# Twelve loads of v, each issued as two transfers: partitions 0 to 119 and partitions 120 to 127

## The chip, the cores and the metric

The kernel runs on one core of one Trainium2 chip. The metric is the device time of one execution in microseconds (us); lower is better. Beside the times there is one profiled execution, whose trace gives the start and length of every instruction, the issue and the completions of every DMA transfer, and what ended each wait.

## The reference, cut to what matters

Two stages follow each other. The first is a gated linear recurrence over 768 positions for each of 4 batches and 8 heads, with a state of 48 by 48. The second takes the result as 3072 tokens of width 384 through two matrix products with a gate g = h cos(h) between them.

```python
f = 1 / (1 + exp(-f_logit))
for t in range(S):                                    # S = 768, per batch and head
    state = f[t][:, None] * state + outer(k[t], v[t])
    y[t] = q[t] @ state
x = y.transpose(0, 2, 1, 3).reshape(3072, 384)
h = x @ w_in                                          # 384 -> 2048
out = (h * cos(h)) @ w_out                            # 2048 -> 384
```

q, k, v and f_logit are four f32 tensors of the same shape (4, 8, 768, 48). The output is 3072 by 384 in f32.

## The kernel before, in words

**Tiling.** The recurrence is cut into 12 pairs (the name n in the code): one pair is 256 positions of one batch, all 8 heads. Within a pair, position 2p + e of the 256 sits on partition p, e = 0 or 1. A load of one of the four inputs for a whole pair is therefore 128 partitions of 8 heads times 96 f32 numbers: on each partition eight runs of 384 bytes, 384 KB in all. For pairs 0 and 1 (HALVES) f, k and q come as two transfers of four heads each, 192 KB apiece; v always comes whole, since VHALVES is empty. The recurrence of a pair is turned into matrix products: running sums of the logarithms of f (step cum), decayed copies of q and k (qm, km), their transposes (qkt), scores (sc) with a mask (am), an inner part (y) and a part from the carried state (yi). After that, units m of 128 or 256 tokens go through the two products of the second stage (h, co, g, o, ot, out).

**What v feeds.** The load of v for pair n (step v*n*) has one reader, step vb*n* in line 400, which casts it to bf16 in the order that the products want. vb runs on ACT for pairs 0 to 2, on DVE for pairs 3 and 11 and on POOL for the others. Readers of vb are the four copies vt (line 404), which feed the inner part y (line 522), and the outer products ps (line 467), which feed the state (st, line 488, and sz, line 494).

**The order of the work.** Nothing is scheduled while the program is built. The string ORDER lists every step by name with its engine (T is PE, S is ACT, V is DVE, G is POOL, Y is SP) and the buffer that it takes; emit walks that list and calls each step. Each engine thus has its instructions in one fixed order and stops at the first whose semaphores are not there. SP only issues transfers: nearly all loads, all transposes of q and k by DMA (step tq, line 414, pairs 4 to 11) and nearly all stores, in one queue. A load whose buffer is still being read waits at the head of that queue with all later ones behind it. Each input has three buffers. Every transfer counts on one of eight completion semaphores, taken in turn over SP's and ACT's transfers, and a transfer waits at its issue for the one eight places before it; readers wait on the semaphore of the transfer that they read.

**Lines.** All loads of f, k, q and v are made by the helper load (lines 294 to 298), whose one DMA instruction stands under line 296. It calls G.step, which notes the name, the engines allowed, the function that issues the instruction and the tile it writes. The fetches of the weights stand in line 282 (step w) and their casts in line 196 (wc, by the helper copy), the first activation on f in line 329 (ex), the products with q and k in lines 337, 345 and 395, the gate of the second stage in line 552 and its products in lines 570 and 586, the stores in line 597.

Of the kernel before, what the change touches and what calls it, by code (L numbers as in the profile page):

```python
# [187 lines left out]
def describe(nc, cpool, ppool, q, k, v, f_logit, moe_w_in, moe_w_out, out):  # L188
    G = Graph()
    eng = lambda e: {"DVE": nc.vector, "POOL": nc.gpsimd, "ACT": nc.scalar, "SP": nc.sync}[e]  # L190
# [65 lines left out]
    p1, p2 = Banks("p1", tiles, 1), Banks("p2", tiles, 2)  # L256
# [36 lines left out]

    def load(name, val, src, b, c, h0, h1):
        tok = src[b, h0:h1, 2 * C * c:2 * C * c + 2 * C, :] if nc is not None else None
        G.step(name, ("SP", "ACT"), lambda e: eng(e).dma_start(  # L296
            out=val.ap.rearrange("p h e d -> p h (e d)"),
            in_=tok.rearrange("h (p e) d -> p h (e d)", e=2)), writes=[val])

    def fetch(kind, pool, src, n, b, c, cut):  # L300

        whole = Val(pool)
        hs = [whole.part(lambda a, u=u: a[:, 4 * u:4 * u + 4]) for u in range(2)]
        if cut:
            for u in range(2):
                load(f"{kind}{n}.{u}", hs[u], src, b, c, 4 * u, 4 * u + 4)
        else:
            load(f"{kind}{n}", whole, src, b, c, 0, H)
        return whole, hs
# [390 lines left out]
```

## Time and profile before

| What | Value |
|---|---|
| Median of 3 runs | 194.66 us |
| The three runs | 196.32, 194.66, 190.06 us |
| The profiled execution | 190.06 us |
| Its span in the trace | 188.3 us |
| Granted TensorE clock, mean | 0.994 |
| Transfers issued | 98 by SP, 6 by ACT |
| Bytes moved by DMA | 34.47 MB in 74395 packets, 67456 of them under 512 B |
| Loads of v | 12 of 384 KB, all by SP, from 2.3 us to 127.8 us |
| Issue of a load of v, min / median / max | 0.379 / 0.943 / 3.577 us |
| Issue to landing of a load of v, min / median / max | 5.3 / 6.5 / 8.1 us |

The profiled execution is the fastest of the three runs. Its span is 1.8 us shorter than its time: what lies around the first and the last instruction. The three runs are 3.3% apart.

How to read what follows: PE is the matrix engine, DVE, ACT and POOL are the three engines for element-wise work, SP the one that issues transfers. SPq is SP's queue: the length of an issue in the trace includes the wait of that instruction for room or for a semaphore, so that an issue of 3.5 us need not be 3.5 us of work. "Landing" is the sixteenth of a transfer's completions: in the trace before, each transfer reports sixteen, at times of their own. An idle time "<- X" was ended by X.

### The profile page before, as it was taken

How to read it: one execution, taken by the hardware profiler on the slowest of the kernel's cores; microseconds unless marked ns; L12 is line 12 of the kernel's file. 1: busy time of each engine (PE TensorE's matmuls, PEld its weight loads, DVE VectorE, ACT ScalarE, POOL GpSimd, SP SyncE). 2: the span in 40 equal slices, each digit the busy share in tenths (PEclk: the TensorE clock that was granted, in tenths of full speed). 3: DMA queues.
4: the chain of work that ended last, by engine and by line, in shares of the span. 5: the costliest groups of instructions: out<-in, count | busy, mean ns of one | idle time of the engine just before them, and what ended most of it. 6: DMA issues, size and time to landing. Idle time of an engine off the chain costs nothing.

```text
span 188.3 us, 5965 instructions
## 1 busy us (share of the span) xinstructions
PE 172.6 (92%) x2523; PEld 123.4 (66%) x2527; DVE 150.0 (80%) x208; ACT 130.7 (69%) x183; POOL 100.6 (53%) x129
## 2 busy tenths in 40 slices
PE   7898658999997999999998999989998999999990
PEld 2464447976666875678566886657667888666660
DVE  4289997998969999898989999989996978633101
ACT  2988775799778899988966989766656774603030
POOL 4538699764498986986457990877833000000000
PEclk9999999999999999999999999999999999999997
DMA  6999999978999599999899899939652000020144
GB/s 146 261 261 270 354 342 309 289 207 244 263 247 253 141 221 255 194 219 209 157 279 282 222 248 201 250 84 166 93 139 87 3 0 0 3 84 0 42 150 146
DMA packets 74395, 34.47 MB, mean 183 GB/s; under 512 B 67456, under 2 KB 72832, under 8 KB 74368
## 3 DMA queue, kind: packets, MB, share of 16 engines
q1 hardware_dynamic: 70944, 32.71, 74.9%
q10 hardware_dynamic: 3424, 1.38, 3.0%
q8 instruction: 20, 0.33, 0.8%
q14 instruction: 7, 0.06, 0.1%
HBM read 25.17 MB, written 4.72 MB: 159 GB/s over the span
## 4 chain that ended last, share of the span: by engine, by line
DVE 40%; PE 36%; DMA 8%; issue 6%; ACT 4%; SPq 3%; POOL 2%; DVEq 0%; ACTq 0%; POOLq 0%
PE ps L570 18%; PE ps L586 14%; DVE am L449 10%; DVE g L552 10%; DVE vt L196 5%; DVE sz L494 4%; DVE st L488 4%; DMA f<-in_f_logit_dram 3%; DMA qkt<-qk 3%; DMA out_dram<-ot 2%; SPq L296 2%; PE ps L522 2%; DVE q L337 2%; DVE qkt L196 1%; DVE x L196 1%
## 5 line engine op out<-in xcount | busy, mean ns | idle before, releaser
L586 PE MATMUL ps<-w_out_bf,g 128*128 128x384 bf16 x384 | 67.9, 327 | 0.4 <-DVE g L552 0.4
L570 PE MATMUL ps<-x,w_in_bf 128*128 128x256 bf16 (+1 forms) x624 | 66.8, 265 | 1.0 <-DVE x L196 0.5
L575 ACT ACTIVATE co<-ps,halfpi 128x1024 bf16<-128x1024 f32 x48 | 52.6, 1113 | 21.7 <-PE ps L570 19.7
L552 DVE TENSOR_TENSOR g<-ps,co 128x1024 bf16<-128x1024 f32 x48 | 60.2, 1303 | 7.9 <-ACT co L575 7.8
L570 PEld LDWEIGHTS <-w_in_bf 128*128 128x128 bf16 x624 | 56.4, 98 | 9.1 <-issue 1.5
L586 PEld LDWEIGHTS <-g 128*128 128x128 bf16 x384 | 36.0, 98 | 23.0 <-DVE g L552 1.2
L449 DVE TENSOR_TENSOR am<-ps,pmask 128x1024 bf16<-128x1024 f32 x24 | 28.6, 1216 | 1.7 <-PE ps L445 0.9
L395 POOL TENSOR_TENSOR qk<-q,b 128x384 bf16<-128x384 f32 x19 | 19.0, 1005 | 8.5 <-DVE q L337 8.3
L395 POOL TENSOR_TENSOR qk<-k,bi 128x384 bf16<-128x384 f32 x21 | 21.7, 1044 | 2.8 <-ACT b L382 1.0
L196 ACT COPY ot<-ps 128x384 f32<-128x384 f32 (+1 forms) x17 | 7.7, 459 | 18.8 <-PE ps L586 9.8
L494 POOL TENSOR_TENSOR sz<-st,b 64x192 bf16<-64x192 f32 x21 | 12.9, 613 | 9.7 <-DVE st L488 8.0
L264 PE MATMUL ps<-zero 128*128 128x512 bf16 x49 | 14.3, 425 | 1.6 <-DVE zero L202 1.2
L196 DVE COPY ot<-ps 128x384 f32<-128x384 f32 (+1 forms) x9 | 4.5, 505 | 12.7 <-PE ps L586 12.3
L345 POOL TENSOR_TENSOR k<-k,f 128x384 f32<-128x384 f32 (+1 forms) x12 | 11.3, 940 | 6.3 <-ACT f L341 4.0
L354 POOL TENSOR_TENSOR sp<-ls 128x384 bf16<-128x384 f32 x8 | 8.0, 1010 | 9.9 <-ACT ls L333 5.0
L488 DVE TENSOR_TENSOR st<-ps,sz 64x192 f32<-64x192 f32 x32 | 11.3, 354 | 1.3 <-issue 0.4
L329 ACT ACTIVATE f<-f 128x768 f32<-128x768 f32 (+1 forms) x14 | 10.4, 748 | 2.2 <-DMA f<-in_f_logit_dram 2.0
L196 DVE COPY vt<-vb 64x384 bf16<-64x384 bf16 x18 | 11.3, 633 | 0.3
L522 PE MATMUL ps<-am,vt 128*32 128x128 bf16 x384 | 7.9, 220 | 3.1 <-DVE am L449 1.6
L445 PE MATMUL ps<-qkt 48*64 48x128 bf16 x384 | 9.2, 220 | 1.6 <-DVE st L488 1.1
L196 POOL COPY vt<-vb 64x384 bf16<-64x384 bf16 x17 | 9.2, 540 | 1.7 <-POOL qk L395 0.9
L445 PEld LDWEIGHTS <-qkt 48*64 48x64 bf16 x384 | 6.2, 106 | 5.2 <-DVE st L488 1.6
(65 smaller groups left out, 178.6 us busy)
## 6 DMA issues: line engine op xcount, KB each, us to landing
v<-in_v_dram SPq DMA_DIRECT2D x12, 384.0 KB, 6.5
out_dram<-ot SPq DMA_DIRECT2D x22, 192.0 KB, 3.3
q<-in_q_dram SPq DMA_DIRECT2D x10, 384.0 KB, 5.8
f<-in_f_logit_dram SPq DMA_DIRECT2D x9, 384.0 KB, 5.7
k<-in_k_dram SPq DMA_DIRECT2D x9, 384.0 KB, 6.1
g<-in_moe_w_in_dram SPq DMA_DIRECT2D x4, 768.0 KB, 7.7
g<-in_moe_w_out_dram SPq DMA_DIRECT2D x4, 768.0 KB, 7.3
k<-in_k_dram SPq DMA_DIRECT2D x4, 192.0 KB, 4.9
```

The lines of the kernel that those rows point to most:

```text
L196: (nc.scalar.copy if e == "ACT" else eng(e).tensor_copy)(out=o, in_=i)
L264: G.step(f"zf{i}", ("PE",), lambda e, dump=dump: nc.tensor.matmul(dump.ap, lhsT=zero[:, 0:128], rhs=zero, start=True, stop=True), writes=[ ...
L395: G.step(f"{nm}{n}.{u}", ("POOL", "DVE"), lambda e, u=u, j=j, src=src, dec=dec: eng(e).tensor_mul(out=qkp[u][j].ap[:, :, :, 0:D], in0=swap ...
L445: nc.tensor.matmul(o[t, r, 2 * a + g, :].rearrange("p (e n) -> p e n", e=2), lhsT=qkv(u)[s, 1, a, g, x, :], rhs=qkv(u)[s, 0, a, g, :, :], ...
L449: G.step(f"am{n}.{u}", ("DVE",), lambda e, u=u, sc=sc: nc.vector.tensor_mul(out=am[u].ap.rearrange("p r b n -> p (r b) n"), in0=sc.ap.rear ...
L488: nc.vector.tensor_add(out=st.ap[s], in0=view()[s], in1=S0.ap[s, :, r, :])
L494: eng(e).tensor_mul(out=new.ap[s, :, r, :].rearrange("p (u a) n -> p u a n", u=2), in0=ap()[s].rearrange("p (u a) n -> p u a n", u=2), in1 ...
L522: nc.tensor.matmul(py[g].ap[32 * c:32 * c + 32, C * m:C * m + C], start=(py[g].first and (g, c) not in begun), stop=(py[g].final and left[ ...
L552: nc.vector.tensor_mul(out=o.rearrange("p b (n e) -> p b e n", e=2), in0=ph.ap.rearrange("p (b e n) -> p b e n", e=2, n=64), in1=co.ap.rea ...
L570: nc.tensor.matmul(ph.ap[:, i * T:(i + 1) * T].rearrange("p (g t) -> p g t", t=C), lhsT=w_in_bf[:, kk, f0:f0 + 128], rhs=xa[:, :, kk, :], ...
L575: G.step(f"co{m}.{j}", ("ACT",), lambda e, ph=ph, co=co: nc.scalar.activation(out=co.ap, in_=ph.ap, func=AF.Sin, bias=halfpi), reads=[ph], ...
L586: nc.tensor.matmul(po.ap[:, 0:DM], lhsT=gT.ap[:, j, i * C:(i + 1) * C], rhs=w_out_bf[:, j, :], start=(po.first and j == 4 * s), stop=(po.f ...
```

## The change

Each load whose step's name begins with v is issued as two DMA instructions one after the other, the first for partitions 0 to 119 and the second for partitions 120 to 127. Both run on the engine that the step has in ORDER, which is SP for all twelve. All other loads stay one instruction over 128 partitions. The tile, its buffers, the bytes and the order of the steps stay as they were; SP's queue has 12 more transfers. Each reader of v now has two completions to wait for instead of one, and the turn of the eight semaphores moves on by two places for a load of v.

```diff
     def load(name, val, src, b, c, h0, h1):
         tok = src[b, h0:h1, 2 * C * c:2 * C * c + 2 * C, :] if nc is not None else None
-        G.step(name, ("SP", "ACT"), lambda e: eng(e).dma_start(
-            out=val.ap.rearrange("p h e d -> p h (e d)"),
-            in_=tok.rearrange("h (p e) d -> p h (e d)", e=2)), writes=[val])
+        parts = ((0, 120), (120, 128)) if name[0] == "v" else ((0, 128),)
+
+        def fill(e):
+            for p0, p1 in parts:
+                eng(e).dma_start(out=val.ap.rearrange("p h e d -> p h (e d)")[p0:p1],
+                                 in_=tok.rearrange("h (p e) d -> p h (e d)", e=2)[p0:p1])
+        G.step(name, ("SP", "ACT"), fill, writes=[val])
```

## The prediction

> **What bounds the kernel now.** I read the page's busy times and chain first, then the stretches, because a share over the span mixes stages; then SP's queue and the tile v, which the change touches. Busy times, DMA busy by slice, DMA queues, the chain by engine, and the issues of v:
>
> ```profile
> PE 172.6 (92%) x2523; PEld 123.4 (66%) x2527; DVE 150.0 (80%) x208; ACT 130.7 (69%) x183; POOL 100.6 (53%) x129
> ...
> DMA  6999999978999599999899899939652000020144
> ...
> q1 hardware_dynamic: 70944, 32.71, 74.9%
> ...
> q8 instruction: 20, 0.33, 0.8%
> ...
> DVE 40%; PE 36%; DMA 8%; issue 6%; ACT 4%; SPq 3%; POOL 2%; DVEq 0%; ACTq 0%; POOLq 0%
> ...
> v<-in_v_dram SPq DMA_DIRECT2D x12, 384.0 KB, 6.5
> ```
>
> The chain runs over DVE and PE; DMA has 8% of it. Yet the transfer engines are at nine tenths for two thirds of the span. The same by stretches (span, then busy time of PE, PEld, DVE, ACT, POOL, the clock, the DMA share and GB/s):
>
> ```profile
> 0.00:62.00 62.00, 53.59 (x871) 36.73 (x876) 51.33 (x89) 48.19 (x76) 42.09 (x57) 1.00 1.06 266
> 62.00:95.00 33.00, 32.42 (x476) 23.96 (x475) 31.66 (x38) 30.29 (x39) 24.98 (x32) 1.00 1.03 196
> 95.00:125.00 30.00, 28.59 (x455) 20.80 (x453) 28.79 (x41) 23.22 (x33) 21.61 (x25) 1.00 1.03 240
> 125.00:145.00 20.00, 19.02 (x444) 14.15 (x441) 17.53 (x23) 13.66 (x20) 11.96 (x16) 1.00 0.58 114
> ```
>
> To 62 us transfers are the scarcest thing beside DVE; from 62 to 125 us DVE and PE are at 95% and more; after 145 us PE is the busy one (38.98 of 43.3 us by the last row, not shown), and no load is left. All loads of v fall before 128 us. The tile v (issues, then who waited for its landing, then issue to landing):
>
> ```profile
> L296 SPq DMA_DIRECT2D v<-in_v_dram x12: 379/943/3577, 2.3 to 127.8; - x12
> ...
>   DMA v<-in_v_dram: 0.2, 1
> ...
>   POOL vb L196: 0.2, 1
> ...
> DMA to landing us min/median/max: 5.3/6.5/8.1
> ```
>
> Only 0.2 us of idle time in the whole span was ended by v itself. And the longest waits of SP's queue to 62 us (total, times, longest):
>
> ```profile
> SPq L282 <- ACT w_out_bf L196: 5.1, 1, 5.1
> SPq L296 <- POOL sp L354: 4.6, 1, 4.6
> SPq L296 <- ACT co L575: 3.0, 1, 3.0
> ```
>
> SP waits for buffers to come free, not for time to issue.
>
> **The issues added.** Twelve transfers on SP. An issue with nothing in its way costs 0.38 us (the shortest of v) to 0.51 us (v0, at 2.33 us); at 0.45 us that is 5.4 us of SP's time. What hides it, load by load from SP's timeline: v0, v1, v3, v4 and v6 are issued while the transfers are the limit: 384 KB land every 1.45 us (48.08, 49.59, 51.09 us), and 5.3 to 8.1 us from issue to landing means three to five transfers queued ahead. After v2 SP waits from 36.8 to 41.9 us for the weights' buffer; after v5 from 59.9 us to 64.4 us for the first transpose; after v7 a store waits for its output until 78.4 us, and the transpose behind it for POOL until 82.9 us. After v8 to v10 the transpose tq8.0 waits for POOL until 110.75 us, and stores ahead of it for DVE until 108.8 us. After v11 tq10.0 waits for POOL until 130.63 us, 1.2 us after its issue. Cost taken: nothing; without that cover 0.45 us each, 5.4 us in all.
>
> The added wait is that of a transfer for the one eight places before it. With v counted twice, eight places hold fewer bytes. I counted places in SP's order against the landings: the tightest are the second part of v9 (waits for k9, landed 98.13 us, due about 98.9 us) and q4 (for v3, 49.59 us, due 50.8 us). Nothing stops; if one did, all of SP's queue behind it would. The second semaphore at vb is a wait of 17 to 30 ns as the trace's other ones are: nothing.
>
> **The transfers themselves.** The bytes and runs of 384 bytes are the same. Does a split cost? The halves of f, k and q (192 KB) land 0.73 to 0.77 us apart (9.14, 9.90, 10.65, 11.42 us), whole loads 1.45 to 1.5 us: time goes with bytes, and two halves cost no more than one whole. So the lower bound by rows is nothing. The upper bound is that the smaller transfer is dealt as badly as can be, and the larger one too, so that some engine carries twice its share: 1.45 us a load. Between them I take one row more on the fullest engine: 128 rows over 16 engines are 8 rows in 1.45 us, a ninth row is 0.18 us. It is near the row of the halves, yet not nothing: a half has 128 rows of four heads and spreads as evenly as a whole, which 120 and 8 rows need not do. A gain is possible only if an engine that is late gets less; that is a rival below.
>
> *By the Trainium skill, page "DMA: Bandwidth & Descriptors", section "Why a DMA increments its semaphore by 16 and not by 1", a transfer runs on the largest number of engines up to 16 that divides its slowest dimension, the lowest-numbered ones: 15 for 120 rows and 8 for 8. Engines 0 to 7 would then carry nine rows, 8 to 14 eight, and the last none, which gives the same 0.18 us; no transfer of before has a count other than 128, so no run here shows it. The same page's "Rules for kernel authors" speaks against the change: disjoint partition ranges share the same engines, and one transfer of 128 partitions is advised; by it the sum is not below nothing.*
>
> **Who feels 0.18 us.** I set each landing of v beside the start of its vb. Seven loads have slack: v2 3.91, v3 1.26, v4 2.16, v6 4.44, v7 2.59, v9 4.35, v10 0.68 us. Four do not: v1 0.20, v5 0.07, v8 0.05, v11 0.09 us; v0 has 0.30 us, but f1.0 two transfers behind it is the chain itself (landing 9.90 us, activation 9.92 us). What queues behind these vb: on ACT the exponentials and tables of the next pair, on POOL qm and km, on DVE (v11) a stretch without idle time to 141 us. Counting all five in full: 5 x 0.18 = 0.9 us. That is generous for v5 and v8, since POOL has 2% of the chain.
>
> Sum, against the profiled execution: 190.06 + 0.9 = 191.0 us. That execution is the fastest of three; set on their median, 194.66 + 0.9 = **195.6 us**, 0.5% slower. I predict on the median. The three runs lie 3.3% apart, so 2% either way is about what can be told from no change.
>
> **Rivals.**
> *The late engine is spared (faster).* After an instruction fetch (q8, 16 KB packets, 1.16 us in the mean) one engine lags: fifteen completions of k1.1 are in by 15.84 us, the last at 17.25 us; for v5 64.10 and 65.23 us; for v8 103.20 and 104.34 us. If the engine that v leaves free is that one, it catches up 1.45 us a load, and the transfers behind land with the rest. For: the fetches take 20 x 1.16 = 23 us of it, v 12 x 1.45 = 17 us, near balance. Against: which engine lags is not in the trace, and the readers concerned sit on POOL. Worth at most the lags where a reader stood ready, 1.41 (k1.1) + 0.96 (w0.3) + 0.84 (k3) + 1.13 + 1.14 = 5.5 us; I take a third, 1.8 us: 192.9 us, down to 189.2. By the skill's rule above it is the sixteenth engine that v leaves free. Chance 0.20, half of it beyond 2%.
> *Fewer engines than I think (slower).* If 120 rows are not dealt out in eights but over 8 engines, those carry 15 or 16 rows, and a load of v takes 2.9 us. It decides from the second load on, where transfers are the limit: the five loads without slack at 1.45 us give 7.3 us, 202.0 us; half of it, where POOL absorbs, 198.3. For: the dealing is unseen. Against: the even landing of all 128-row transfers, which gives no sign of a costly dealing. Chance 0.18.
> *SP becomes the limit (slower).* Half of the 5.4 us of issues reach the path, at the transposes that share the queue: the chain waits for one in full (133.03 us, 4.87 us, qkt). 195.6 + 2.7 = 198.3 us. Against: the waits listed above. Chance 0.15, two thirds of it beyond 2%.
> *The change does nothing* (each vb waits for something else): 194.7 us; it is in my forecast.
>
> **How the numbers follow.** Forecast 0.47, of which 0.34 within 2%, 0.06 faster and 0.07 slower by the scatter of the runs. Faster 0.06 + 0.10 = 0.16; slower 0.07 + 0.18 + 0.10 = 0.35; within 2% the rest, 0.49. The forecast's own range is 190.06 + 0.9 to 196.32 + 0.9: 191.0 to 197.2 us. The range goes down to 190.5 us (most of the spared engine) and up to 200.5 us (SP, and the cheaper half of fewer engines), leaving out about 2 in 10.
>
> **What would show it.** SP's view of the load line: 24 issues of v, unblocked ones at 0.4 to 0.5 us; if some stay over 1 us at the second part, room in the queue is what is short. Transfers of v landing 0.2 us later against their neighbours confirm the ninth row, 1.4 us the fewer engines; a last completion no longer late by a microsecond behind a fetch, the spared engine. The idle time ended by v should stay under 1 us. I am wrong if waits "SPq <- DMA" appear, if ACT or DVE waits for v by microseconds, or if the transposes land later than 5 us.

## The result and the profile after

| | Before, measured beside it | After |
|---|---|---|
| Median | 190.15 us (19 executions) | 194.99 us (19 executions) |
| Lowest to highest | 189.18 to 196.32 us | 191.00 to 198.56 us |
| Ratio after / before | | 1.0113, 95% interval 1.0068 to 1.0157 |
| Profiled execution, its span | 190.06 us, 188.3 us | 197.03 us, 195.3 us |
| Granted TensorE clock, mean | 0.994 | 0.982 |

The ratio leaves out executions far above the quickest of their own kernel, of which after has many more than before. By the ratio the change costs 1.1%, some 2.1 us; by the medians 4.8 us. The profile after lies in the upper part of its times, so I read it for what can go wrong, and a second profile of the same kernel (192.57 us) beside it. The changed file is four lines longer: L296 is now L300, and L467, L494, L552 and L570 are L471, L498, L556 and L574.

The page of the changed kernel: busy times, the granted clock and the DMA share in 40 slices, the transfer queue (packets, MB, share of 16 engines), the chain by engine, and the issues of v (count, KB, us to landing).

```profile
PE 177.1 (91%) x2527; PEld 126.3 (65%) x2527; DVE 153.6 (79%) x208; ACT 131.2 (67%) x183; POOL 100.1 (51%) x129
...
PEclk9999988999998899999999999999999999999999
DMA  6999999976999999996389999995956000020152
...
q1 hardware_dynamic: 71028, 32.71, 75.7%
...
PE 37%; DVE 28%; DMA 21%; POOL 4%; ACT 3%; issue 3%; SPq 1%; DVEq 0%; ACTq 0%; POOLq 0%
...
v<-in_v_dram SPq DMA_DIRECT2D x12, 360.0 KB, 7.6
```

The same bytes move, but DMA's share of the chain has gone from 8% to 21%, and the larger part of v lands 7.6 us after its issue (the median) where whole loads took 6.5. The clock row has two dips, at slices 6 and 7 and at 13 and 14. The same by stretches (columns as in the prediction: span, busy times, clock, DMA share, GB/s):

```profile
0.00:62.00 62.00, 53.52 (x848) 35.95 (x849) 49.69 (x83) 47.15 (x74) 39.29 (x53) 0.97 1.07 248
62.00:95.00 33.00, 29.94 (x426) 22.68 (x427) 30.78 (x38) 24.82 (x33) 23.62 (x30) 0.95 0.91 196
95.00:125.00 30.00, 28.75 (x436) 21.18 (x437) 27.78 (x36) 25.72 (x33) 19.35 (x24) 1.00 1.06 206
```

To 62 us the transfer engines are as busy as before (1.07 against 1.06) and move 248 GB/s in place of 266. PE lost 2.5 us of work between 62 and 95 us (29.94 against 32.42 us busy). The tile v (issues, then what ended the idle time before its readers, who waited for it, and issue to landing):

```profile
L300 SPq DMA_DIRECT2D v<-in_v_dram x24: 295/882/3814, 2.3 to 136.2; - x24
...
  DMA v<-in_v_dram: 4.2, 5
...
  PE ps L471: 2.5, 2
  ACT vb L196: 2.4, 2
  POOL vb L196: 1.9, 3
...
DMA to landing us min/median/max: 5.9/7.6/9.9
```

The last line holds only the parts whose completions the view can count off; read from all completions, the twelve 120-row parts take 5.0 to 9.9 us, with the same median of 7.6. Before, 0.2 us of idle time in one place was ended by v; now 4.2 us in five. SP's own waits to 62 us, by contrast, have hardly moved (total, times, longest), and no wait of SP's for a transfer is among the longest:

```profile
SPq L282 <- ACT w_out_bf L196: 6.1, 1, 6.1
SPq L300 <- POOL sp L358: 4.1, 1, 4.1
SPq L300 <- ACT f L333: 2.5, 2, 1.4
SPq L300 <- ACT co L579: 1.8, 1, 1.8
```

**Landings**, read from the completions in the two traces, in us; both parts must have landed:

| Transfer | v0 | q0.0 | f1.0 | v1 | k1.1 | v2 | v3 | v4 | v6 | v5 | v8 |
|---|---|---|---|---|---|---|---|---|---|---|---|
| Before | 8.41 | 9.14 | 9.90 | 15.14 | 17.25 | 39.71 | 49.59 | 55.42 | 56.72 | 65.23 | 104.34 |
| After | 9.28 | 9.84 | 10.60 | 17.75 | 18.20 | 42.40 | 53.14 | 59.89 | 62.19 | 69.85 | 112.79 |

q0.0 and f1.0, the whole transfers behind the first split one, are each 0.70 us late. That is four times the 0.18 us of the prediction, by the first load alone.

**Where the time came in.** The end of the first, 10th, 16th, 25th and 46th of the 48 gates on DVE (g, L556), in us, in the traces of these kernels (the last two are experiments below):

| Profile | 1st | 10th | 16th | 25th | 46th | Time |
|---|---|---|---|---|---|---|
| Before | 33.1 | 64.6 | 83.0 | 110.0 | 163.6 | 190.06 |
| After | 35.2 | 68.8 | 90.2 | 117.2 | 171.0 | 197.03 |
| The changed kernel again | 31.8 | 67.0 | 86.2 | 113.2 | 166.8 | 192.57 |
| After, one multiply moved | 33.6 | 66.1 | 84.8 | 111.8 | 165.9 | 192.48 |
| The same, TensorE's gaps filled | 32.7 | 65.5 | 84.1 | 111.1 | 165.4 | 191.16 |

The whole loss of after is there by the 16th gate: 2.1 us by 33 us, 2.1 more by 69 us, 3.0 more by 90 us. Behind that the two kernels run in step.

### The profile page after: what moved, and what is told of

Its sections match the earlier page's. It is cut to its first block, busy times and chain, and to the rows that moved or that the text cites. A ratio compares the mean times of both kernels' runs of the same rounds, so it can differ in the third digit from the quotient of the medians.

```text
span 195.3 us, 5981 instructions
## 1 busy us (share of the span) xinstructions
PE 177.1 (91%) x2527; PEld 126.3 (65%) x2527; DVE 153.6 (79%) x208; ACT 131.2 (67%) x183; POOL 100.1 (51%) x129
## 4 chain that ended last, share of the span: by engine, by line
PE 37%; DVE 28%; DMA 21%; POOL 4%; ACT 3%; issue 3%; SPq 1%; DVEq 0%; ACTq 0%; POOLq 0%
PE ps L574 18%; PE ps L590 12%; DMA v<-in_v_dram 8%; DVE g L556 8%; DVE am L453 6%; DMA qkt<-qk 6%; DMA f<-in_f_logit_dram 5%; DVE sz L498 4%; DVE vt L196 4%; DMA out_dram<-ot 3%; POOL qk L399 2%; PE ps L264 2%; DVE st L492 2%; ACT co L579 2%; PE ps L449 1%
## 5 line engine op out<-in xcount | busy, mean ns | idle before, releaser
L574 PE MATMUL ps<-x,w_in_bf 128*128 128x256 bf16 (+1 forms) x624 | 69.9, 272 | 1.0 <-DVE x L196 0.6
L556 DVE TENSOR_TENSOR g<-ps,co 128x1024 bf16<-128x1024 f32 x48 | 60.2, 1303 | 9.4 <-ACT co L579 9.3
L574 PEld LDWEIGHTS <-w_in_bf 128*128 128x128 bf16 x624 | 58.7, 101 | 10.1 <-issue 1.8
L498 POOL TENSOR_TENSOR sz<-st,b 64x192 bf16<-64x192 f32 x21 | 12.1, 575 | 12.6 <-DVE st L492 8.5
L264 PE MATMUL ps<-zero 128*128 128x512 bf16 x53 | 16.1, 439 | 1.2 <-DVE zero L202 1.2
L196 DVE COPY vt<-vb 64x384 bf16<-64x384 bf16 x18 | 11.8, 662 | 0.3
L498 DVE TENSOR_TENSOR sz<-st,b 64x192 bf16<-64x192 f32 x11 | 11.9, 1082 | 0.2
```

What stands on the lines that cost most here:

```text
L196: (nc.scalar.copy if e == "ACT" else eng(e).tensor_copy)(out=o, in_=i)
L264: G.step(f"zf{i}", ("PE",), lambda e, dump=dump: nc.tensor.matmul(dump.ap, lhsT=zero[:, 0:128], rhs=zero, start=True, stop=True), writes=[ ...
L498: eng(e).tensor_mul(out=new.ap[s, :, r, :].rearrange("p (u a) n -> p u a n", u=2), in0=ap()[s].rearrange("p (u a) n -> p u a n", u=2), in1 ...
L556: nc.vector.tensor_mul(out=o.rearrange("p b (n e) -> p b e n", e=2), in0=ph.ap.rearrange("p (b e n) -> p b e n", e=2, n=64), in1=co.ap.rea ...
L574: nc.tensor.matmul(ph.ap[:, i * T:(i + 1) * T].rearrange("p (g t) -> p g t", t=C), lhsT=w_in_bf[:, kk, f0:f0 + 128], rhs=xa[:, :, kk, :], ...
```

## Experiments: is it the second transfer, or leaving out partitions?

My theory at this point: a transfer that leaves partitions out takes longer than its bytes. The rivals: SP's extra issue and the second semaphore cost the time, or one engine carries a ninth row.

**The changed kernel again**, for a profile at another granted clock.

> The changed kernel once more, beside the two other splits below on the same chip. Measured so far: 1.0113 of the kernel before (0.7% to 1.6% slower), where 1.005 was forecast. Three theories. Engine count: the 120-row transfer, on 15 engines, moves its rows more slowly than a 128-row transfer on 16 does (in the trace of the changed kernel q0.0 and f1.0, behind v0, land 0.70 us later than before, not 0.18). Second issue: it is the second transfer as such, its issue of 0.4 us in SP's queue and its place among the eight semaphores. Ninth row: a load costs 0.18 us as forecast, and the rest is scatter. All three expect 1.007 to 1.016 here, that is 191.5 to 193.5 us beside 190.2 us; the profile should show q0.0 landing about 9.8 us again, against 9.14 us before.

Measured: median 193.44 us (10 executions, 188.88 to 197.81) against 189.74 us of before; ratio 0.9999 (0.9945 to 1.0053). Its profile took 192.57 us at clock 1.00, q0.0 landing at 9.87 us. So the late landing repeats, but the ratio does not, and its interval does not overlap that of the result: it differs from call to call by as much as the 1.1% that it showed. The medians lie above before in both calls, by 4.8 and 3.7 us.

**Split at 64, and at 112.**

```diff
-        parts = ((0, 120), (120, 128)) if name[0] == "v" else ((0, 128),)
+        parts = ((0, 64), (64, 128)) if name[0] == "v" else ((0, 128),)
```

> Each load of v as partitions 0 to 63 and 64 to 127: the second issue and the semaphore places stay, but both parts can use 16 engines with four rows each. Engine count and ninth row expect the time of before, 0.998 to 1.003, and q0.0 landing at 9.1 to 9.3 us. Second issue expects what the changed kernel has, 1.007 to 1.016.

> Each load of v as partitions 0 to 111 and 112 to 127: one large and one small part as in the change, but seven rows and one row on each of 16 engines. Engine count expects 0.998 to 1.003, if it is the 15 engines that cost; if any transfer that isn't a power of two of rows is slow, the 112 rows take longer than 1.3 us and the ratio lies at 1.005 to 1.016. Second issue expects 1.007 to 1.016. Ninth row expects 0.998 to 1.003.

Measured: 194.16 us (188.30 to 199.19, 10 executions) and 195.44 us (190.78 to 198.13, four executions) against 189.74 us. q0.0 lands at 9.64 and 9.45 us, 0.50 and 0.31 us behind before. Both are as slow as the split at 120. Every part of these two reports sixteen completions, and 112 rows are seven for each of 16 engines, 64 are four; so the loss needs neither a ninth row nor an engine left out.

**The same bytes in two transfers of all 128 partitions**, heads 0 to 3 and heads 4 to 7.

```diff
-        parts = ((0, 120), (120, 128)) if name[0] == "v" else ((0, 128),)
+        parts = ((0, 4), (4, 8)) if name[0] == "v" else ((0, h1 - h0),)
...
-            for p0, p1 in parts:
-                eng(e).dma_start(out=val.ap.rearrange("p h e d -> p h (e d)")[p0:p1],
-                                 in_=tok.rearrange("h (p e) d -> p h (e d)", e=2)[p0:p1])
+            for a0, a1 in parts:
+                eng(e).dma_start(out=val.ap.rearrange("p h e d -> p h (e d)")[:, a0:a1],
+                                 in_=tok.rearrange("h (p e) d -> p h (e d)", e=2)[:, a0:a1])
```

> Each load of v as two transfers of all 128 partitions, heads 0 to 3 and heads 4 to 7 (192 KB each): the second issue and the turn of the semaphores are those of the change, but no transfer leaves out partitions. So far: the change, 64 and 64 rows, and 112 and 16 rows all have a median of 193 to 195 us beside 189.7 us, so that the number of engines alone isn't it. Theory partial rows: a transfer of fewer than 128 partitions takes more than its share of the queue (alone: 1.21 us for 128 rows, 1.62 us for 120, 1.85 us for 120 and 8, 1.67 us for 64 and 64); it expects the time of before here, median 189 to 191 us, and q0.0 landing at 9.1 to 9.3 us. Theory second issue: SP's queue and the semaphores; it expects 193 to 196 us.

Measured: 190.37 us (189.28 to 191.85, 12 executions) against 190.57 us, ratio 1.0002 (0.9962 to 1.0042). The tile v and the clock of this run:

```profile
L300 SPq DMA_DIRECT2D v<-in_v_dram x24: 375/653/3210, 2.3 to 128.3; - x24
...
  DMA v<-in_v_dram: 1.3, 2
...
DMA to landing us min/median/max: 3.2/5.2/6.9
```

As many issues, as many semaphores and turns as in the changed kernel, and no loss. v0 lands at 8.17 and q0.0 at 8.92 us, 0.2 us ahead of before. SP's issues are cleared; the cost lies in leaving partitions out.

**Transfers alone.** Loads of the same sources and shapes in groups of six, with nothing else running but a copy per tile that keeps the groups apart.

> The transfers by themselves, with no compute but a copy that frees each buffer: groups of six loads of 128 rows, 120 rows (0 to 119), 112 rows, 8 rows, 120 and 8 rows, 64 and 64 rows, 120 rows (8 to 127) and 64 rows. None of the reference's computation is done. It gives the time from one landing to the next in a full queue. Engine count expects 1.45 us for 128 rows, 2.0 to 2.3 us for 120 rows, 1.3 us for 112 rows, 2.1 to 2.4 us for 120 and 8, 1.45 us for 64 and 64. Ninth row expects 1.45 us for 120 rows, 1.6 us for 120 and 8. If 120 rows from partition 8 on are as slow as from 0, it is the number of engines, and not which partitions they hold.

> Transfers alone again, none of the computation is done: groups of six loads of 128 rows, two transfers of four heads each, 112 and 16 rows, 120 and 8, 120, 104, 88, 96 and 32 rows. 104 and 88 rows fill 13 and 11 engines with eight rows each, as 120 rows fill 15. If each engine is slow by itself (eight rows that aren't spread as in a 128-row transfer), 120, 104 and 88 rows all take 1.6 us; if the engines hinder each other, fewer rows take less: 104 rows 1.4 us, 88 rows 1.2 us. Two transfers of four heads take 1.2 to 1.25 us a load; 112 and 16 rows 1.5 to 1.7 us, as 64 and 64 did.

Measured, from landing to landing within a group, where the steps are steady (the first and last of some groups are longer):

| Rows in one load | First run | Second run |
|---|---|---|
| 128 | 1.21 us | 1.21 us |
| 128, two transfers of four heads | | 0.60 us each, 1.21 us |
| 120 + 8 | 1.82 to 1.99 us | 1.86 us |
| 112 + 16 | | 1.55 us |
| 64 + 64 | 0.83 us each, 1.67 us | |
| 120 | 1.62 us | 1.49 to 1.63 us, median 1.58 |
| 120, rows 8 to 127 | 1.54 to 1.76 us | |
| 112 | 1.25 us | |
| 104 | | about 1.4 us |
| 96 | | 1.40 us |
| 88 | | 1.2 to 1.5 us |
| 64 | 1.04 us | |
| 32 | | 0.2 to 0.5 us |
| 8 | 0.2 to 0.6 us | |

In the second run's page the rate in 40 slices of 2.33 us shows the step: whole loads and loads by heads first, then 112 + 16, and from the 13th slice on 120 + 8 and the other partial ones. The 365 GB/s near the end are stores.

```profile
DMA  1999999999999999999999986789999941999994
GB/s 18 294 325 321 323 324 324 308 261 251 254 219 222 220 229 219 219 231 227 223 211 220 228 191 186 218 195 211 219 210 197 120 88 59 365 368 368 365 366 166
```

The engines report themselves as busy until the loads of 88 rows, at 325 GB/s with whole loads and at some 220 with 120 rows. So a split load costs 1.86 - 1.21 = 0.65 us, of which some 0.3 us is the smaller transfer itself (1.86 - 1.58). What inside the transfer engines makes 120 or 96 rows slower than 128 stays open: 104 and 88 rows go to fewer engines (thirteen and eleven completions) and take less time than 120, so it is not the number of engines alone, and no run here shows which partitions each engine is given.

**Only the first three, and only the last nine.**

```diff
-        parts = ((0, 120), (120, 128)) if name[0] == "v" else ((0, 128),)
+        parts = ((0, 120), (120, 128)) if name in ("v0", "v1", "v2") else ((0, 128),)
```

> Only v0, v1 and v2 are split at 120, the other nine are whole. In the change everything is 0.7 us late from 10 us on and 2.2 us late at 42 us. If the early loads are what counts, since transfers are the limit there, about half to two thirds of the loss is here: median 191.5 to 194 us, and vb1 again 2 us later than before (15.34 us). If the loss comes from the loads after 42 us, 189.5 to 190.5 us.

> Only v3 to v11 are split at 120, the first three are whole. If the early loads are what counts: median 190 to 191.5 us. If the loads of 42 to 62 us (v3, v4, v6, v5) are: 192 to 195 us, with the wait of PE for vb4 (1.34 us before, 2.25 us after) at 2 us or more.

Measured: the first three alone 194.94 us (six executions: 187.85 and 188.51 us at a clock of 0.997 or more, 194.79 to 196.42 us at 0.991 or less) against 190.57 us; the last nine alone 195.04 us (12 executions, 191.22 to 197.44), ratio 1.0072 (1.0020 to 1.0124). Each alone comes to the median of all twelve. The loss of the medians is no sum over loads, then. Something that either can set off adds some 4 us or does not.

## Experiments: what is set off

Sorted by granted clock, all executions of before in five calls and of the changed kernel in two:

| Granted clock | Before: executions, median | The changed kernel: executions, median |
|---|---|---|
| 0.994 and more | 47, 189.8 us | 9, 191.1 us |
| 0.985 to 0.993 | 45, 191.0 us | 12, 194.7 us |
| under 0.985 | 7, 195.4 us | 8, 197.4 us |

Above 193 us lie 11 of 99 executions of before and 19 of 29 after. The clock and the time go together, but in the middle row the changed kernel loses 3.7 us at the same clock: the clock is not all.

**The clock.** Stretches of the changed kernel's trace (span, busy PE, PEld, DVE, ACT, POOL, clock, DMA share, GB/s):

```profile
24.28:27.69 3.41, 1.69 (x47) 1.00 (x45) 3.21 (x6) 3.32 (x7) 3.41 (x3) 1.00 1.05 368
27.69:31.11 3.42, 3.42 (x38) 3.14 (x31) 3.11 (x3) 0.58 (x1) 3.27 (x4) 0.50 1.18 277
58.41:61.82 3.41, 1.16 (x43) 0.93 (x41) 2.58 (x5) 2.95 (x5) 3.25 (x4) 1.00 1.16 218
61.82:65.24 3.42, 3.42 (x36) 2.38 (x24) 2.88 (x5) 1.11 (x1) 2.60 (x5) 0.50 0.88 209
```

After 3.41 us in which PE was busy for 1.69, and again for 1.16 us, comes a stretch of 3.42 us at half clock with PE busy throughout: an estimate of up to 1.7 us of matmul time lost each time. Before has no half clock until 186 us. PE's gap ahead of the outer products of pair 4, in the timeline of after (start, us, what, idle before and its releaser), is 2.25 us; in before it is 1.34 us, with the same releaser. After, then before:

```profile
61.54 0.46 PE L471 MATMUL ps<-vb,qk 64*64 64x48 bf16 x32 [2.25 <-POOL vb L196]
...
58.59 0.44 PE L467 MATMUL ps<-vb,qk 64*64 64x48 bf16 x32 [1.34 <-POOL vb L196]
```

That is v4, landed at 59.89 us and cast at 60.54 us: a load that the prediction had put down as having 2.16 us of slack. By the Trainium skill, page "TensorE: Matmul & The Clock Gate", section "Part 1: The HAM clock gate (the "warmup" mystery)", the clock is set by a free-running window of 3413 ns and goes to half after an idle one; the 3.42 us agree. The rule of the same page's section "Why this matters for your kernels", against PE-idle gaps of more than some 3 us, is too lax for this trace, where no gap before either stretch exceeds 2.25 us.

Before, too, has a stretch of 3.4 us, from 24.3 us on, with PE 0.45 busy, and nothing follows. The traces say why. In each of them the changes of clock lie whole numbers of 3.413 us apart (after: 27.69, 31.11, 61.82 and 65.24 us), so that the edges of the windows can be counted from them. In before, counted back from its drop at 186.07 us, an edge falls inside that stretch, and each of the two windows that share it has enough work:

```profile
22.24:25.65 3.41, 2.49 (x53) 1.39 (x52) 3.21 (x5) 2.85 (x6) 3.41 (x4) 1.00 1.04 379
25.65:29.06 3.41, 2.45 (x52) 2.36 (x53) 3.35 (x5) 1.68 (x2) 3.27 (x4) 1.00 1.21 295
```

Counted so in the 17 traces of the whole kernel, the ends of the spans left out, half clock follows ten of the eleven windows with PE busy half of the time or less, one of the seven at 0.51 to 0.56, and none above. And the stretch near 28 us does not need the split loads: before with a multiply moved (the run is below; the order is that of before up to some 80 us) has it too, behind a window from 24.60 us on with PE busy for 1.69 us. Where the edges fall differs from execution to execution, so this part of the scatter is in both kernels; what the late v4 adds is the longer gap near 60 us.

To test it, zero matmuls in the gaps: five ahead of the ps step of pair 4, five ahead of y of pair 0, five more around cum3 and sc1.1; the same in the kernel before; and the changed kernel with six more ahead of the second half of h5.3.

```diff
+    def idle(ap, count):
+        for _ in range(count):
+            nc.tensor.matmul(ap, lhsT=zero[:, 0:128], rhs=zero, start=True, stop=True)
...
         def outer(e, u):
+            if n == 4 and u == 0:
+                idle(ps[0].ap, 5)
...
         def inner(e):
+            if n == 0:
+                idle(py[0].ap, 5)
```

> The changed kernel with 17 more 128x512 matmuls of zeros on TensorE (0.2 to 0.27 us each by the rows of the changed kernel: 3 in 0.82 us, 5 in 1.24 us), put where TensorE stands still: 5 ahead of the ps step of pair 4 (gap 59.29 to 61.54 us), 5 ahead of the y step of pair 0 (gap 20.43 to 21.86), 2 and 3 more around the cumulative sums of pair 3 and ahead of sc1.1 (gaps of 0.64 and 1.09 us up to 27.34). v is still split at 120. Theory 'half clock': the larger part of the loss is stretches of 3.4 us at half clock that follow a half-idle 3.4 us; with the gaps filled the stretches near 27 and 61 us go from the profile, the mean granted clock is 0.99 or more in most executions, and the median falls from 195 to about 191.5, with what is left (some 1.5 us) the cost of the late transfers alone. Rival 'transfers alone': the half clock is only a sign of the waiting and costs nothing by itself; the median stays at 194 to 196 and no lower than that of the changed kernel.

> The kernel before with the same 17 matmuls of zeros in the same places, v whole. Theory 'half clock': the median is that of before within 0.5 us (189.5 to 190.6), and executions above 192 us, which before has about one in five of, become rarer; if the added matmuls delay real ones (the gap ahead of pair 4's ps step is only 1.34 us here, 5 matmuls take 1.24) it may lose up to 0.3 us. Rival 'transfers alone': the same median and the same share of executions above 192 us as before.

> As the first run of this call, and 6 more zero matmuls ahead of the second half of h5.3 (some 1.3 us), so that the gap of 2.79 us at 87.46 us, which in other runs of split loads was followed by a half-clock stretch at 88 us, is shorter too. Theory 'half clock': no half-clock stretch before the end in the profile, a median 0 to 1 us below that of the first run. Rival 'transfers alone': equal to the changed kernel or up to 1.3 us above it, the time of the added matmuls.

| | Median | Executions | Before beside it |
|---|---|---|---|
| After, three gaps filled | 192.90 us | six: 192.2 to 193.2, then 196.9 and 200.0 | 190.77 us |
| Before, the same | 190.72 us | 12, 189.8 to 195.3 | 190.77 us |
| After, the fourth gap too | 192.77 us | six, 191.0 to 193.3 | 190.77 us |

(The expectations count 17 matmuls; there are 15.) With all four gaps filled no execution has a clock under 0.996, none is above 193.3 us, and the median falls by 2.2 us against that of after. The upper group is gone when the clock stays. But the median of the first run was to be 191.5 and is 192.9 us, and before with the same matmuls still goes to 195.3 us. One more thing is in it.

**A held multiply.** In before with zero matmuls, at 194.15 us, TensorE has a gap of 2.96 us at 84 us, and after has one of 2.79 us at 87 us. Both stand behind one small DVE instruction and the gate that follows it. DVE and then POOL in after:

```profile
84.55 1.21 DVE L453 TENSOR_TENSOR am<-ps,pmask 128x1024 bf16<-128x1024 f32 x1
85.78 3.08 DVE L498 TENSOR_TENSOR sz<-st,b 64x192 bf16<-64x192 f32 x1
88.90 2.51 DVE L556 TENSOR_TENSOR g<-ps,co 128x1024 bf16<-128x1024 f32 x2
```

```profile
84.98 0.99 POOL L399 TENSOR_TENSOR qk<-q,b 128x384 bf16<-128x384 f32 x1
85.93 1.00 POOL L349 TENSOR_TENSOR k<-k,f 128x384 f32<-128x384 f32 x1
86.87 0.82 POOL L196 CAST vb<-v 128x768 bf16<-128x768 f32 x1
87.66 0.99 POOL L399 TENSOR_TENSOR qk<-k,bi 128x384 bf16<-128x384 f32 x1
```

The same multiply and its neighbours on POOL in before:

```profile
81.21 0.40 DVE L494 TENSOR_TENSOR sz<-st,b 64x192 bf16<-64x192 f32 x1
```

```profile
80.40 0.99 POOL L395 TENSOR_TENSOR qk<-q,b 128x384 bf16<-128x384 f32 x1
81.91 1.00 POOL L345 TENSOR_TENSOR k<-k,f 128x384 f32<-128x384 f32 x1 [0.53 <-DMA k<-in_k_dram]
```

In before POOL waits 0.53 us for a load of k, and the multiply ends in that gap, at 81.61 us. In after POOL arrives late, the load is there, four instructions follow each other without a gap, and the multiply ends at 88.86 us, 0.21 us after the last of them. The other profiles fit. Wherever the multiply stands, it ends 0.21 to 0.23 us after the end of a POOL instruction. It is held for 3.1 to 3.4 us in four more (split at 112, the first three, the last nine, before with zero matmuls; 194.2 to 196.7 us), each time to the end of the same four. It takes 0.4 to 0.7 us in the six others that run it there, four of which have a gap of 0.7 to 0.9 us on POOL there, as before has one of 0.53; two have next to none (0.01 and 0.04 us), and the five that hold it have none at all. But other multiplies of the same line do get in between two POOL instructions without a gap (in before the one at 130.99 us), so what decides is open. The multiply reads two inputs from SBUF; am and g, with one from PSUM, run beside POOL at their usual 1.2 us. The Trainium skill knows of such contention: page "GPSIMD Engine Reference", section "8. Key points", has POOL share its SBUF interfaces with VectorE, with contention for DVE instructions with two SBUF inputs, and page "Trainium Architecture — The Big Picture", section "What this means for kernel authors", calls it an exclusive lock. The trace agrees, with 3.08 us against 0.40; that a hold lasts through four POOL instructions is what this trace adds.

The multiply was moved to POOL, next to its twin, in the changed kernel, in before, and in the changed kernel with the zero matmuls of the first run above:

```diff
-h5.01:T am5.0:V0 sz5.01:V1 zsz.3:G vt6.3:G qm6.1:G co4.0:S3 co5.0:S2 vt5.1:S h5.30:T4 h5.31:T
-sz5.00:G qm6.0:G g4.0:V g5.0:V2 ...
+h5.01:T am5.0:V0 zsz.3:G vt6.3:G qm6.1:G co4.0:S3 co5.0:S2 vt5.1:S h5.30:T4 h5.31:T
+sz5.01:G1 sz5.00:G qm6.0:G g4.0:V g5.0:V2 ...
```

> The changed kernel with one step moved: the state multiply sz5.01, which DVE runs at 85.78 us in 3.08 us, goes to POOL ahead of its twin sz5.00 (0.50 us there). Theory 'hold': the multiply was held by four POOL instructions in a row (0.99, 1.00, 0.82 and 0.99 us from 84.98 us on), g and yi of pair 5 came 2.4 us late by it, and TensorE's gap of 2.79 us at 87.46 us with the half clock that may follow came from it; so the gap goes, and the median falls by 1.5 to 3 us, to 192 to 193.5, with the half-clock stretches at 27 and 61 us left. Rival 'lateness': the gap is made by late inputs and only shows at this instruction; TensorE waits as long at 84 to 90 us for another step and the median stays at 194 to 196.

> The kernel before with the same step moved to POOL. Theory 'hold': executions of 193 us and more, which before shows in 3 of 17 to 4 of 23, become rare, and the others are unchanged within 0.3 us or lose up to 0.5 us to the added POOL instruction; median 189.5 to 190.5. Rival: they are as frequent as before, or the added POOL time costs 0.5 us or more everywhere.

> The changed kernel with the same step moved and the 17 zero matmuls in TensorE's gaps at 20 to 27 and at 59 us. Theory 'hold and half clock': no executions above 193 us, a granted clock of 0.995 or more before the end, median 190.5 to 192 us; what is left above the kernel before (0.5 to 1.5 us) is the late transfers and the zero matmuls themselves. Rival: a tail above 194 us remains, so that something else makes it, or the median stays at that of the run with the zero matmuls alone (192.8 to 192.9 us).

| | Median | Lowest to highest | Before beside it |
|---|---|---|---|
| After, multiply moved | 192.90 us (6) | 191.68 to 194.81 | 190.42 us |
| Before, multiply moved | 191.07 us (12) | 189.21 to 192.67 | 190.42 us (highest 197.91) |
| After, moved and gaps filled | 192.81 us (12) | 190.56 to 194.57 | 190.42 us |

In the profile of the first of them TensorE has no gap there any more:

```profile
81.43 3.53 PE L574 MATMUL ps<-x,w_in_bf 128*128 128x256 bf16 x30
84.89 0.52 PE L526 MATMUL ps<-qkt,sz 128*32 128x128 bf16 x24
```

The median of after falls by 2.1 us, as the theory of the hold had it. Before has nothing above 192.7 us, but with 11 of 99 above 193 us otherwise, 12 executions would show none about one time in four, so it is not shown that its tail is gone. Its median is 0.65 us higher, more than I gave it, though its ratio of 1.0018 (0.9987 to 1.0050) does not tell that from nothing. The third run is a half miss: no granted clock under 0.996 and nothing above 194.6 us, but the median is 192.8 us, not 190.5 to 192. Its executions fall in two groups, 190.6 to 191.3 (five) and 192.5 to 194.6 us (seven), all at full clock, and the profile at 191.16 us lies in the lower. I ran the kernel twice more for a profile of the upper group.

> The run before once more (multiply moved, zero matmuls, v split at 120), for a profile. Theory 'another hold': if this execution is above 192.4 us at full clock, a DVE instruction with two inputs from SBUF or of the fast kind takes 2 us or more above its usual time beside POOL instructions without a gap, and TensorE has a gap behind it that the profile at 191.16 us has not. Rival 'late transfers': no such instruction, and v or k lands 2 us later against its reader than in the profile at 191.16 us. Below 191.5 us it tells nothing new.

> As the run ahead of it, for a second chance at an execution above 192.4 us: a held DVE instruction of 2 us or more (theory 'another hold') or a landing 2 us later against its reader (rival 'late transfers').

They came at 192.38 and 192.11 us, between the groups; neither has a held instruction, and at most of the gates both lie 0.3 to 1.1 us behind the quicker profile. What the upper group is stays open.

None of these mends touches the ratio to before: 1.0116 with the multiply moved, 1.0111 and 1.0102 with three and four gaps filled and 1.0075 with both, beside 1.0113 for after, each give or take some 0.005. They take away the highest executions; about 1% stays in these calls (the changed kernel's second call showed none), and what makes it was not isolated.

**Does a kernel beat both?** The two quick executions of the first-three run were 1.3% below before (0.9870, 0.9796 to 0.9944). So: only v0 to v2 split, and zero matmuls in the gaps but that of pair 4.

> Only v0, v1 and v2 split at 120, as in the earlier run with the first three loads alone, and zero matmuls in TensorE's gaps as in the last call: 5 ahead of y of pair 0, 2 and 3 more around the sums of pair 3 and ahead of sc1.1, 6 ahead of the second half of h5.3; none ahead of pair 4, whose v is whole. The earlier run stood at 187.9 to 188.5 us where its granted clock was 0.997 or more and at 194.8 to 196.4 in its other four executions. Theory 'half clock': with no half-clock stretch before the end all executions come to 188.5 to 190.5 us, at or below the kernel before. Rival: the added matmuls cost what the run with the gaps of all loads filled showed at full clock (192.8 against 191.1 us, 1.7 us), and the median is 190 to 191.5 us, no faster than the kernel before. If executions of 194 us and more remain, something other than these gaps makes the half clock in this kernel.

Measured: 192.27 us (12 executions, 189.59 to 193.00, all at 0.996 or more) against 190.37 us, ratio 1.0033 (0.9992 to 1.0074). No execution came to 188.5 us. None of these kernels beats before.

## Why the prediction was wrong, by its own steps

- **The issues and the second semaphore, "cost taken: nothing": right.** As many issues by heads cost nothing (ratio 1.0002), and SP's waits are still for buffers.
- **The transfer term, 0.18 us a load: wrong, and the step that failed first.** It took a full row as the unit of time. (The three landings it quotes are 1.50 us apart, not 1.45; a row would be 0.19 us, which changes nothing.) A split load takes 0.65 us more alone and put q0.0 back by 0.70 us. The upper bound of 1.45 us holds. The row that I leaned on, halves of f, k and q at 0.73 to 0.77 us, was of transfers over all 128 partitions, and told nothing of 120; my caution that "120 and 8 rows need not" spread as evenly pointed the right way. The Trainium skill's rule weighed there (page "DMA: Bandwidth & Descriptors", section "Rules for kernel authors"), one transfer of 128 partitions, is borne out, though its reason, shared engines, does not cover halves by heads, which share them too and cost nothing. That page's count of engines agrees: a 120-row transfer reports fifteen completions, an 8-row one eight, each beside one record at its issue's end.
- **Who feels it, five loads of twelve: wrong.** Slack was read as fixed. But the queue adds up the lateness: v3 lands 3.6, v4 4.5 and v6 5.5 us later. v4 had 2.16 us and became the end of a TensorE gap of 2.25 us.
- **The sum, 0.9 us: wrong by what it has no term for.** By the ratio the loss is 2.1 us in one call and nothing in the next, with 0.9 us between the two; by the medians it is 4.8 and 3.7. Of these the held multiply is about 2 (moving it: 194.99 to 192.90 us, in another call). Filling four gaps gives 2.2 us, but not on top: hold, gap and half clock are one chain, since the gap behind the hold was followed by a half-clock stretch in three of the five traces with a hold. Some 2 to 2.5 us are left with either, of which the nine executions at a clock of 0.994 or more show 1.2 (191.1 against 189.8).
- **The number.** 195.6 us is close to the 194.99 measured only because it was set on the median of three runs, 194.66 us; with 19 executions that median is 190.15. That is luck. The distance from before, 0.9 us, is what was wrong.
- **The rivals.** The spared engine: false; the completion late by 1.9 us is still there in v4's 120-row part (14 in by 58.02 us, the last at 59.89). Fewer engines: false as told, fifteen and eight being in use, but its mechanism, a load of v that takes more of a queue that is the limit, is what happened, at under half its price. SP as the limit: false.
- **"I am wrong if ACT or DVE waits for v by microseconds": it did**, 2.4 us on ACT and 2.5 us on PE.

## What to carry to other kernels

Split a load along the free dimension, over all 128 partitions, if it has to be split; here a transfer of 120, 96 or 64 rows took more time for its bytes than one of 128 (1.6, 1.40 and 1.04 us against 1.21), and such a price can be measured alone, where one run settles it. Where transfers are the limit, a small price is paid by every later load, so slack has to be compared with the lateness added up to that point. A kernel with tight gaps has steps in its time: look in the timeline for DVE instructions of two SBUF inputs beside unbroken POOL work and for 3.4 us with PE half idle, and compare distributions, not one execution.

## What I had not expected of the hardware

- 120 rows of 3 KB take 1.6 us and 128 rows 1.21 us, back to back; 96 rows take 1.40 us; by the slices 120 rows move some 220 GB/s against 325, with the engines reported busy in both.
- A DVE multiply of 0.40 us took 3.08 to 3.39 us beside unbroken POOL instructions, and its end followed the last of them by 0.21 us.
- Half clock for 3.42 us came after 3.41 us in which PE was busy for 1.69 us, with no single gap above 1.09 us. A stretch as idle, but shared by two windows (2.49 and 2.45 us busy), was followed by none.
